# Layer 2, tiles 9 and 15: the residual of the expert output as an identity product on TensorE and a ScalarE copy, in place of a VectorE addition

## The chip, the cores and the metric

One core of one Trainium2 chip. The time is that of the device for one execution of the whole program, in microseconds (us); of several runs the median is given. The engines are called TensorE (PE in profile rows, PEld for its weight loads), VectorE (DVE), ScalarE (ACT), GpSimd (POOL) and SyncE (SP, which issues all DMA transfers here).

## The reference

Two kinds of layer alternate on x of 2048 rows by 576 columns: linear attention (32 heads) and a mixture of tiny experts. Each works on a layer-normed x and is added to x. The whole is done twice.

```python
x = x + _A_ref(_layernorm(x, axis=-1), A_wqkv, A_wo)
x = x + _B_ref(_layernorm(x, axis=-1), B_w_q, B_k1, B_k2, B_u, B_v)
x = x + _A_ref(_layernorm(x, axis=-1), A_wqkv, A_wo)
x = x + _B_ref(_layernorm(x, axis=-1), B_w_q, B_k1, B_k2, B_u, B_v)
```

The expert part, per row of x (xf is the normed row), with one expert chosen per head:

```python
q = jnp.einsum("nd,dhc->nhc", xf, w_q)
s1 = jnp.einsum("nhd,ed->nhe", q[..., :dk], k1)
s2 = jnp.einsum("nhd,ed->nhe", q[..., dk:], k2)
# best of 8 in s1 and best of 8 in s2 name one of 64 experts
act = _gelu(jnp.einsum("nd,nhkd->nhk", xf, u[top_e]))
out = jnp.einsum("nhk,nhk,nhkd->nd", g, act, v[top_e])   # g is 1: K = 1
```

The change concerns the last of the four additions, x + _B_ref, for two of the sixteen groups of rows.

## The kernel before

The 2048 rows are 16 tiles of 128. A tile goes through a number of steps, each a Python generator that is advanced piece by piece (`yield` is the boundary of a piece). In the program text, `play` holds the order as a written list: `po1.9` advances step `po` (exp_out) of layer 2 (the kernel counts layers 0 and 1), tile 9, by one piece; `x2` behind a word means two pieces. Within a part of that list, `in_order` keeps each of TensorE, ScalarE, VectorE and GpSimd to exactly that order: what stands behind a waiting instruction on its engine waits too. SyncE's queue of transfers follows its own order.

The last steps of a tile of layer 2, with the words of the list and the names in the rows:

- `O` (back_out, L483, tile ppo): TensorE multiplies the attention output by its weights, 28 matmuls. VectorE adds x in `residual` (L473) and writes x1 along with its row sum. ScalarE squares x1 (L188, junk); GpSimd makes mean and scale (L187 to L195, mb and rsb); ScalarE writes the normed row, yb (L205).
- `bc` (exp_T): TensorE transposes yb of one tile together with the expert weights cg of an earlier tile (L215, ptb: five transposes and one). ScalarE copies them out as thib (L117) and VectorE makes the rest, tlob (L118), so that products of float32 precision are made of two parts. So `bc1.12,10` transposes yb of tile 12 and cg of tile 10.
- `S` (exp_scores, L525, pps): 14 matmuls give the scores; ScalarE copies them to s (L530).
- `gel` and `sel`: ScalarE and GpSimd make the gelu, g (L539 to L545); VectorE picks the experts in a row of small operations (L553 to L590, mt to cg).
- `po` (exp_out, L609, tile po): four matmuls multiply the transposed cg by the table vmix. What remains is to add x1 and to store the result x2 to `out` (L623).

The last addition has two forms. Without a `base` step, VectorE does it in `residual` (L473), reading po and x1 and writing x2. With a `base` step ahead (exp_base, L598), TensorE first multiplies x1 by the identity matrix into the same accumulator po, the four matmuls of L609 add to it, and ScalarE copies the sum to x2 (L613). Before the change, tiles 10, 11 and 12, the last three, have this second form. All other tiles have the first.

Accumulators come from a pool `ps` of four buffers; x2 has a pool of two, so an addition or a copy waits until the output transfer of the tile before the last is done.

Of the kernel before, what the change touches and what calls it, by code (L numbers as in the profile page):

```python
# [64 lines left out]
def network(ctx, tc, x_in, wqkv, wo, wq_t, k_t, u_t, v2, c_mask, c_mask4, c_ident, c_code, c_code1, c_scale, c_shift, out):  # L65
# [90 lines left out]
    @contextmanager  # L156
    def in_order(*engines):

        ins = nc.cur_bb.bb.instructions
        last = ins[-1]  # L160
        yield
        ins = nc.cur_bb.bb.instructions
        start = next(i for i in reversed(range(len(ins))) if ins[i] is last) + 1
        for e in engines:
            mine = [i for i in ins[start:] if i.engine == e]
            for x, y in zip(mine, mine[1:]):
                tc.add_manual_dep(y, x.name, mybir.DependencyInfo(mybir.DependencyClass.NoSync, mybir.DependencyReason.DATA),
                                  reason="in_order")
# [587 lines left out]
    def play(text, at=0):  # L756

        for w in text.split():
            f, l, t, c, n = re.fullmatch(r"([A-Za-z]+)(\d)\.(-?\d+)(?:,(-?\d+))?(?:x(\d+))?", w).groups()
            run(int(l), (pieces[f], (at + int(t), at + int(c)) if c else at + int(t), int(n or 1)))  # L760
# [114 lines left out]
    with in_order(*ALL):  # L875

        play("""
            bT0.13 gel0.12 po0.11 sel0.12 v1.10 po0.11x2 gel0.12 num0.15 sel0.12 k1.10 bT0.13 v1.10 sel0.12 fT1.11
            sel0.12 oT0.14 v1.10 fT1.11 O0.14 num0.15 cT0.12 num0.15 k1.10 cT0.12 O0.14 oT0.15 bT0.13 po0.12 S0.13
            O0.14 fT1.11 S0.13 oT0.15 po0.12x3 sel0.13x2 v1.11 gel0.13 fT1.12 gel0.13 oT0.15 O0.14 sel0.13x2 k1.11  # L880
            v1.11 O0.15 fT1.12 O0.15 bT0.14 st1.10 cT0.13 v1.11 bT0.14 S0.14 cT0.13 O0.15 fT1.12 keep1.12 po0.13 k1.11
            S0.14 gel0.14 sel0.14 po0.13 gel0.14 st1.11 po0.13 k1.12 sel0.14x2 po0.13 fT1.13 k1.12 O0.15 v1.12x2
            sel0.14 v1.12 bT0.15 cT0.14x2 st1.12 fT1.13 bT0.15 po0.14 S0.15 po0.14 fT1.13 S0.15 po0.14 ldx1.1 po0.14
            ldx1.3 v1.13 fT1.14 v1.13 sel0.15x3 gel0.15 k1.13 fT1.14 gel0.15 bT0.-1 v1.13 sel0.15 cT0.15 v1.14 cT0.15
            po0.15 k1.13 q1.13 bT0.-1 po0.15 q1.13 v1.14 po0.15x2 v1.14 k1.14 wl1.0 st1.13 fT1.15x2 k1.14 k1.15 v1.15
            rl1.0 st1.14 k1.15 ldq1.13 v1.15x2 rl1.2 st1.15 lq1.0 mk1.0 zs1.0 M1.1 rl1.1 lq1.0 M1.1 rl1.3 ldx1.0 zs1.0
            M1.4x2 M1.3 lq1.1 M1.0 num1.13 num1.0 num1.13 num1.0x2 M1.3 keep1.11 lq1.1 num1.1 M1.0 oT1.0x2 num1.1
            M1.2x2 rl1.4 num1.1 num1.13 lq1.2 O1.0 oT1.1 oT1.13 q1.14 lq1.2 O1.0 oT1.1 O1.0x2 num1.2 q1.14 lq1.3x2
            num1.2 oT1.13 bc1.0,-9 num1.3 O1.1 bc1.0,-9 num1.2 S1.0 O1.1 oT1.2 S1.0 num1.3 lq1.4 gel1.0 num1.3 oT1.2
            O1.1x2 O1.2 bc1.1,-9 sel1.0 gel1.0 ldx1.2 sel1.0 lq1.4 O1.13 rl1.6 bc1.1,-9 sel1.0 num1.4x2 S1.1 O1.2x2  # L890
            ldx1.13 O1.13 S1.1 lq1.6 O1.2 sel1.0 sel1.1 bc1.2,0 rl1.5 ldx1.5 rl1.7 num1.4 oT1.3 ldq1.14 lq1.5 lq1.6
            gel1.1 bc1.2,0 oT1.4 gel1.1 sel1.1 O1.13 rl1.8 sel1.1 S1.2 po1.0 oT1.3 lq1.5 sel1.1 S1.2 O1.3 po1.0 sel1.2
            rl1.9 O1.13 oT1.4 num1.6 bc1.13,1 num1.5 sel1.2 num1.5 lq1.7 bc1.13,1 gel1.2x2 num1.5 S1.13 O1.3 lq1.7
            O1.3x2 num1.6 rl1.11 sel1.2 po1.1 oT1.5 q1.15 oT1.5 ldx1.4 sel1.2 bc1.3,2 po1.1 S1.13 gel1.13 num1.6 O1.4
            bc1.3,2 sel1.13 q1.15 ldx1.6 po1.2 O1.5 oT1.6 ldq1.15 po1.2 sel1.13 num1.14 S1.3 O1.4 lq1.8 O1.4 num1.14
            num1.7 rl1.10 sel1.13 gel1.13 O1.5 num1.14 O1.4 num1.7 S1.3 sel1.13 ldx1.7 sel1.3 oT1.6 num1.7 bc1.4,13
            ldx1.14 bc1.4,13 rl1.12 O1.6 ldx1.8 lq1.8 po1.13 O1.5 gel1.3 O1.5 sel1.3 oT1.7 po1.13 sel1.3 num1.8 O1.6
            S1.4 gel1.3 num1.8 oT1.7 S1.4 sel1.3 sel1.4 gel1.4 sel1.4 oT1.14 bc1.5,3 lq1.9 O1.6 sel1.4 bc1.5,3 S1.5
            po1.3 ldx1.15 O1.6 num1.8 ldx1.11 gel1.4 oT1.8 oT1.14 num1.15 S1.5 sel1.4 bc1.6,4 po1.3 sel1.5 gel1.5
            lq1.9 bc1.6,4 num1.15 O1.14 num1.9 oT1.8 S1.6 O1.14x2 sel1.5 O1.14 S1.6 gel1.5 po1.4 num1.15 sel1.5x2 O1.7  # L900
            po1.4 num1.9 gel1.6 bc1.14,5 O1.7 bc1.14,5 oT1.15 gel1.6 O1.7 sel1.6 num1.9 O1.8 po1.5 S1.14x2 O1.7 po1.5
            oT1.9 sel1.6 O1.8 sel1.6 ldx1.9 O1.8 sel1.6 sel1.14 gel1.14 oT1.15 sel1.14 lq1.10 oT1.9 lq1.10 bc1.7,6x2
            O1.9 gel1.14 O1.8 sel1.14 po1.6 ldx1.10 po1.6 num1.10 S1.7x2 sel1.14 num1.10 O1.9 sel1.7 bc1.8,14 num1.10
            lq1.11 bc1.8,14 po1.14 sel1.7 O1.9 lq1.11 O1.9 gel1.7x2 sel1.7 S1.8 sel1.7 O1.15 S1.8 ldx1.12 gel1.8
            sel1.8 num1.11 po1.14 O1.15 oT1.10 bc1.9,7 gel1.8 sel1.8 bc1.9,7 lq1.12 O1.15 S1.9 sel1.8 oT1.10 num1.11
            sel1.8 lq1.12 O1.15 num1.12 po1.7 S1.9 num1.11 bc1.15,8 gel1.9 po1.7 sel1.9 O1.10 gel1.9 oT1.11 num1.12
            bc1.15,8 O1.10x2 po1.8x2 sel1.9 oT1.11 S1.15x2 sel1.9 O1.11 O1.10 gel1.15 sel1.9 gel1.15 sel1.15 bc1.10,9
            num1.12 O1.11 sel1.15 bc1.10,9 O1.11 oT1.12 S1.10 sel1.15 po1.9 O1.11 sel1.15 oT1.12 S1.10 gel1.10
            bc1.11,15 sel1.10 O1.12 po1.9 gel1.10 bc1.11,15 O1.12x2 S1.11 sel1.10x2 po1.15 sel1.10 po1.15 S1.11
            sel1.11 O1.12 sel1.11 base1.10 bc1.12,10x2 gel1.11x2 sel1.11 S1.12x2 sel1.11 base1.11 gel1.12 sel1.12  # L910
            gel1.12 po1.10 bc1.-1,11x2 base1.12 sel1.12x2 po1.10 sel1.12 po1.11x2 bc1.-1,12x2 po1.12x2
        """)
# [44 lines left out]
```

## Time and profile before

| | |
|---|---|
| runs | 719.56, 718.05, 720.6 us; median 719.56 us |
| profiled execution | 718.14 us, its span 716.4 us |
| granted TensorE clock, mean | 0.996 |
| TensorE busy | 699.6 us (98%) |
| VectorE busy | 475.1 us (66%) |
| ScalarE busy | 321.6 us (45%) |
| GpSimd busy | 201.6 us (28%) |
| identity products L598, weight loads and matmuls | 12 each, 697.7 to 706.5 us |
| ScalarE copies L613 | 3, of 0.65 us each |

The span runs from the first to the last instruction; the time of the execution has 1.74 us more. A busy share says how long an engine had work, not whether the end waited for it. In rows of the timeline the columns are start, duration, engine, line, operation, output and inputs, shapes, count, and in brackets the idle time of that engine just before with what ended it. The mean over all stages hides that the last 30 us have few tiles left to overlap.

### The profile page before, as it was taken

What the parts mean: (1) busy time and instruction counts of PE and PEld (TensorE: products, weight loads), DVE (VectorE), ACT (ScalarE), POOL (GpSimd) and SP (SyncE); (2) the same over time, 40 slices, a digit from 0 to 9 for tenths busy, and PEclk for the clock granted to TensorE, in tenths of its full rate; (3) what the DMA queues carried; (4) which work ended last, traced back from release to release, by engine and by line L of the source; (5) the groups of instructions that cost most, each with busy time, mean ns of one, the idle gap of its engine ahead of it and who ended that gap; (6) DMA issues with size and microseconds to landing.
All of it is one profiled execution on the core that took longest, in us unless ns stands there. A gap on an engine that the chain in (4) does not pass through costs nothing.

```text
span 716.4 us, 14695 instructions
## 1 busy us (share of the span) xinstructions
PE 699.6 (98%) x5464; PEld 650.7 (91%) x5464; DVE 475.1 (66%) x1031; ACT 321.6 (45%) x658; POOL 201.6 (28%) x543
## 2 busy tenths in 40 slices
PE   9999999999999999999999999999999999999995
PEld 6999989999998999899998999899899999899984
DVE  5533343435437877688787888551647788988996
ACT  5422422343224456455565554644544534454442
POOL 3211000111004533334443433210323234434431
PEclk9999999999999999999999999999999999999998
DMA  9847777765302322566767665514532324111101
GB/s 270 291 164 243 266 234 262 247 192 175 108 1 64 103 101 91 162 216 215 245 218 233 212 196 175 168 44 128 149 120 84 97 86 125 47 67 34 67 17 66
DMA packets 82711, 107.17 MB, mean 150 GB/s; under 512 B 8976, under 2 KB 47376, under 8 KB 82640
## 3 DMA queue, kind: packets, MB, share of 16 engines
q1 hardware_dynamic: 82640, 106.24, 46.5%
q8 instruction: 43, 0.70, 0.4%
q14 instruction: 28, 0.23, 0.1%
HBM read 68.88 MB, written 37.32 MB: 148 GB/s over the span
## 4 chain that ended last, share of the span: by engine, by line
PE 82%; DVE 8%; ACT 4%; issue 2%; DMA 2%; POOL 1%; SPq 0%; DVEq 0%; ACTq 0%; POOLq 0%
PE ppk L258 15%; PE ppv L258 14%; PE ppq L258 14%; PE ppo L483 12%; PE pps L525 7%; PE kva L525 5%; PE kva L360 3%; PE fold_ps L641 2%; PE po L609 2%; PE ptb L215 2%; PE m L414 1%; PE pto L215 1%; DVE x L473 1%; PE ppq L270 1%; PE ppk L270 1%
## 5 line engine op out<-in xcount | busy, mean ns | idle before, releaser
L483 PE MATMUL ppo<-ohi,thio 126*128 126x252 f32 (+1 forms) x320 | 50.5, 300 | 2.6 <-ACT thio L117 2.6
L483 PEld LDWEIGHTS ppo<-ohi,thio 126*128 126x128 f32 (+1 forms) x320 | 44.8, 189 | 4.4 <-ACT thio L117 3.1
L258 PE MATMUL ppk<-whi,thif 128*128 128x252 f32 (+1 forms) x300 | 45.3, 298 | 0.8 <-ACT thif L117 0.8
L188 ACT ACTIVATE junk<-x,mb 128x576 bf16<-128x576 f32 x32 | 24.8, 775 | 45.2 <-POOL mb L187 44.9
L453 POOL TENSOR_TENSOR o<-pq,zb 128x576 f32<-128x576 f32 x19 | 27.4, 1441 | 62.2 <-ACT zb L399 58.6
L258 PE MATMUL ppv<-whi,thif 128*128 128x252 f32 (+1 forms) x300 | 44.7, 295 | 0.1
L258 PEld LDWEIGHTS ppk<-whi,thif 128*128 128x128 f32 x300 | 40.9, 188 | 4.0 <-issue 2.9
L205 ACT ACTIVATE yb<-x,rsb 128x640 f32<-128x640 f32 x32 | 29.5, 921 | 33.3 <-POOL rsb L195 33.3
L179 POOL TENSOR_SCALAR rsf<-mvf 128x1 f32<-128x1 f32 x16 | 3.4, 212 | 145.3 <-DVE mvf L176 145.2
L258 PE MATMUL ppv<-whi,tlof 128*128 128x252 f32 (+1 forms) x300 | 43.9, 293 | 0.0
L258 PE MATMUL ppk<-whi,tlof 128*128 128x252 f32 (+1 forms) x300 | 43.9, 293 | 0.0
L258 PEld LDWEIGHTS ppv<-whi,thif 128*128 128x128 f32 x300 | 41.3, 188 | 1.0 <-issue 0.4
L258 PEld LDWEIGHTS ppk<-whi,tlof 128*128 128x128 f32 x300 | 41.2, 188 | 0.0
L258 PEld LDWEIGHTS ppv<-whi,tlof 128*128 128x128 f32 x300 | 41.2, 188 | 0.0
L483 PE MATMUL ppo<-olo,thio 126*128 126x252 f32 (+1 forms) x256 | 39.6, 293 | 0.0
L258 PE MATMUL ppq<-whi 128*128 128x252 f32 (+1 forms) x260 | 39.5, 299 | 0.0
L483 PE MATMUL ppo<-ohi,tloo 126*128 126x252 f32 (+1 forms) x256 | 39.4, 293 | 0.0
L277 DVE TENSOR_SCALAR ek<-ek 128x576 f32<-128x576 f32 x16 | 7.3, 457 | 46.4 <-ACT ek L276 46.4
L258 PEld LDWEIGHTS ppq<-whi 128*128 128x128 f32 x260 | 36.0, 188 | 0.6 <-DVE eq L287 0.3
L483 PEld LDWEIGHTS ppo<-olo,thio 126*128 126x128 f32 x256 | 36.2, 188 | 0.0
L483 PEld LDWEIGHTS ppo<-ohi,tloo 126*128 126x128 f32 x256 | 36.1, 188 | 0.0
L258 PE MATMUL ppk<-wlo,thif 128*128 128x252 f32 x240 | 36.1, 293 | 0.0
(205 smaller groups left out, 1784.6 us busy)
## 6 DMA issues: line engine op xcount, KB each, us to landing
fold<-in_wq_t SPq DMA_DIRECT2D x64, 288.0 KB
whi<-hl_d SPq DMA_DIRECT2D x26, 320.0 KB
y_df<-rf SPq DMA_DIRECT2D x23, 320.0 KB
gf<-y_df SPq DMA_DIRECT2D x92, 80.0 KB
pq_d<-eq SPq DMA_DIRECT2D x19, 288.0 KB
pq<-pq_d SPq DMA_DIRECT2D x19, 288.0 KB
xf<-in_x SPq DMA_DIRECT2D x16, 288.0 KB
x<-in_x SPq DMA_DIRECT2D x16, 288.0 KB
```

Of the source, the lines that this page charges most:

```text
L188: nc.scalar.activation(junk, xt, AF.Square, bias=m[:, 0:1], accum_out=m[:, 1:2])
L205: nc.scalar.activation(y, x2, AF.Identity, scale=rs[:, 0:1], bias=rs[:, 1:2])
L215: nc.tensor.transpose(pt[:, b * P:(b + 1) * P], x, ident)
L258: nc.tensor.matmul(o[:, at:at + c1 - c0], tt[a == "lo"][:, b, :], wb[:, cols + c0:cols + c1], start=(i == 0), stop=(i == len(todo) - 1))
L270: nc.tensor.matmul(p[:, at:at + c1 - c0], tt[a == "lo"][:, b, :], wb[:, cols + c0:cols + c1], start=(i == 0), stop=(i == len(todo) - 1))
L277: nc.vector.tensor_scalar(e, e, 1.0, EPS, op0=ALU.min, op1=ALU.add)
L360: nc.tensor.matmul(a[64 * h:64 * h + 64, c * 72:c * 72 + n], vt[:, 2 * c + h], fk[:, f0:f0 + n], start=(t == 0 and c == 0), stop=(t == NT ...
L453: nc.gpsimd.tensor_tensor(o[:, :D], pq, zb, op=ALU.mult)
L483: nc.tensor.matmul(p[:, at:at + c1 - c0], hl[a][:r, b], w[:r, c0:c1], start=(i == 0), stop=(i == len(todo) - 1))
L525: nc.tensor.matmul(p[:, :512], hl[a == "lo"][:, b, :], shi[:, b] if w == "hi" else slo[:, blocks(REM)[b][1]], start=(i == 0), stop=(i == l ...
L609: nc.tensor.matmul(p[:, at:at + c1 - c0], c[i], vmix[:, c0:c1], start=(i == 0 and not based), stop=(i == 1))
L641: nc.tensor.matmul(p[32 * j:32 * j + 32, at:at + c1 - c0], kpad[:, ch // 2, 24 - 8 * a:56 - 8 * a], st[:, c0:c1], start=(a == 0), stop=(a ...
```

## The change

Two words are added to the list: `base1.9` directly ahead of `po1.9`, and `base1.15` directly ahead of `po1.15`. exp_out then finds a base and takes its second form for tiles 9 and 15.

```diff
-            num1.12 O1.11 sel1.15 bc1.10,9 O1.11 oT1.12 S1.10 sel1.15 po1.9 O1.11 sel1.15 oT1.12 S1.10 gel1.10
-            bc1.11,15 sel1.10 O1.12 po1.9 gel1.10 bc1.11,15 O1.12x2 S1.11 sel1.10x2 po1.15 sel1.10 po1.15 S1.11
+            num1.12 O1.11 sel1.15 bc1.10,9 O1.11 oT1.12 S1.10 sel1.15 base1.9 po1.9 O1.11 sel1.15 oT1.12 S1.10 gel1.10
+            bc1.11,15 sel1.10 O1.12 po1.9 gel1.10 bc1.11,15 O1.12x2 S1.11 sel1.10x2 base1.15 po1.15 sel1.10 po1.15 S1.11
```

Per tile this adds two instructions in the program on TensorE (each becomes two weight loads and two matmuls in the trace), removes one addition with its row sum from VectorE, and adds one copy on ScalarE.

In the instruction order, names carry the tile in the middle (`po_15_9296` is po of tile 15). TensorE around tile 15, before; pps_11 are the scores of tile 11, ptb_12 the transposes of tile 12:

```order
L525 MATMUL pps_11_9266<-shi,tlob_11_9214 128x512 x5
L609 MATMUL po_15_9296<-vmix,thib_11_9213 128x252
L609 MATMUL po_15_9296<-vmix,thib_11_9213 128x324
L609 MATMUL po_15_9296<-vmix,tlob_11_9214 128x252
L609 MATMUL po_15_9296<-vmix,tlob_11_9214 128x324
L598 MATMUL po_10_9331<-x_10_9020,ident 128x252
L598 MATMUL po_10_9331<-x_10_9020,ident 128x324
L215 MATMUL ptb_12_9334<-ident,yb_12_9322 128x128 x5
```

And after:

```order
L525 MATMUL pps_11_9267<-shi,tlob_11_9216 128x512 x5
L598 MATMUL po_15_9297<-x_15_8830,ident 128x252
L598 MATMUL po_15_9297<-x_15_8830,ident 128x324
L609 MATMUL po_15_9297<-vmix,thib_11_9215 128x252
L609 MATMUL po_15_9297<-vmix,thib_11_9215 128x324
L609 MATMUL po_15_9297<-vmix,tlob_11_9216 128x252
L609 MATMUL po_15_9297<-vmix,tlob_11_9216 128x324
L598 MATMUL po_10_9333<-x_10_9020,ident 128x252
L598 MATMUL po_10_9333<-x_10_9020,ident 128x324
L215 MATMUL ptb_12_9336<-ident,yb_12_9324 128x128 x5
```

The identity product of tile 15 now stands between the scores of 11 and po of 15; that of tile 9 stands likewise between the scores of 10 and po of 9.

ScalarE from the gelu of tile 10 to thib of tile 12, before:

```order
L539 ACTIVATE g_10_9202<-s_10_9174 128x64
L543 ACTIVATE g_10_9202<-g_10_9202 128x64
L117 ACTIVATE thib_11_9213<-ptb_11_9206 128x768
L188 ACTIVATE junk,mb_12_9263<-x_12_9260,mb_12_9263 128x576
L530 ACTIVATE s_11_9281<-pps_11_9266 128x512
L205 ACTIVATE yb_12_9322<-x_12_9260,rsb_12_9318 128x640
L117 ACTIVATE thib_12_9341<-ptb_12_9334 128x768
```

And after:

```order
L539 ACTIVATE g_10_9204<-s_10_9174 128x64
L613 ACTIVATE x_9_9253<-po_9_9182 128x576
L543 ACTIVATE g_10_9204<-g_10_9204 128x64
L117 ACTIVATE thib_11_9215<-ptb_11_9208 128x768
L188 ACTIVATE junk,mb_12_9264<-x_12_9261,mb_12_9264 128x576
L613 ACTIVATE x_15_9309<-po_15_9297 128x576
L530 ACTIVATE s_11_9282<-pps_11_9267 128x512
L205 ACTIVATE yb_12_9324<-x_12_9261,rsb_12_9320 128x640
L117 ACTIVATE thib_12_9343<-ptb_12_9336 128x768
```

The copy of tile 9 stands between the two gelu operations of tile 10, the copy of tile 15 ahead of s of 11 and yb of 12. On VectorE the addition of tile 9 is gone from between the selection of 10 (m_10) and tlob of 11, that of tile 15 from between cg of 10 and mt of 11. SyncE's queue keeps its order; the transfers of tiles 9 and 15 now wait for ScalarE.

## The prediction

> **What bounds the kernel now.** I read the page's chain of work that ended last first.
>
> ```profile
> PE 82%; DVE 8%; ACT 4%; issue 2%; DMA 2%; POOL 1%; SPq 0%; DVEq 0%; ACTq 0%; POOLq 0%
> ```
>
> TensorE is the bound over the whole run. The change, though, touches only the last 30 us, so what matters is that stretch, and there I read the chain in order of time (start, duration, engine, tile, line).
>
> ```profile
> 659.22 3.66 PE ppo L483 x28
> ...
> 689.02 0.54 PE po L609 x4
> 689.56 0.66 PE ptb L215 x6
> 690.22 0.04 issue
> 690.25 3.92 PE ppo L483 x28
> 694.18 3.27 PE pps L525 x14
> 697.45 0.53 PE po L609 x4
> 697.99 0.97 PE po L598 x4
> 698.96 0.88 PE ptb L215 x6
> ...
> 699.92 0.82 ACT thib L117
> 700.74 0.04 issue
> 700.78 3.56 PE pps L525 x14
> ...
> 712.59 0.65 ACT x L613
> ```
>
> The first row is for comparison. By the program's order the pieces from 689.02 on are po of tile 9, ptb of 11, ppo of 12, pps of 11, po of 15, the identity product (L598) of tile 10, ptb of 12, thib of 12, pps of 12 and, after s and the selection of 12, the last copy. Two things are to be seen. From 689 to 699.8 TensorE runs without a gap worth naming: whatever is inserted there is paid. From ptb of 12 on, each step waits for the one before it (transposes, ScalarE's thib, scores, ScalarE's s, VectorE's selection, output): whatever delays ptb of 12 delays the end by the same amount. Both identity products of the change go into the first stretch, and both copies onto the engine that has to feed ptb of 12.
>
> ScalarE's own rows around the place, in order of time, with its idle time in brackets:
>
> ```profile
> 691.83 0.26 ACT L543 ACTIVATE g<-g 128x64 f32<-128x64 f32 x1 [1.34 <-POOL g L541]
> 691.99 0.80 ACT L117 ACTIVATE thib<-ptb 128x768 fp32r<-128x768 f32 x1
> ...
> 697.49 0.60 ACT L530 ACTIVATE s<-pps 128x512 f32<-128x512 f32 x1 [1.21 <-PE pps L525]
> 697.98 0.91 ACT L205 ACTIVATE yb<-x,rsb 128x640 f32<-128x640 f32 x1
> ```
>
> The s at 697.49 is that of tile 11; it starts when pps of 11 ends. The yb at 697.98 is tile 12's normalized input, and its end at 698.89 is what ptb of 12 begins on. ScalarE takes its rows in order: thib of 11 had its transposes at 690.22 (chain) and still stood until 691.99, behind a g that waited for GpSimd.
>
> **The change, part by part.** *Identity product of tile 9, TensorE.* In the chain an identity product is one piece of 0.97 us (697.99). It goes ahead of po of 9: po ends at 689.02 + 0.97 + 0.54 = 690.53, ptb of 11 at 691.19. Before, ppo of 12 stood 0.04 us for ScalarE's s of 10 and then took 3.92 us; the piece at 659.22, which follows its predecessor without a wait, took 3.66, and I take 3.68. That wait is over by 691.19, so ppo of 12 ends at 691.19 + 3.68 = 694.87 in place of 694.18: of the 0.97 us, 0.69 remain.
>
> *Copy of tile 9, ScalarE, and its addition off VectorE.* In ScalarE's order it stands between the two g rows of tile 10. It can start at about 690.57 and takes 0.65 us (the copy at 712.59); the second g did not start before 691.83, since GpSimd was late. It fits in that 1.34 us gap: nothing. It would begin to cost if po of 9 came over 0.6 us later still. On VectorE the addition goes:
>
> ```profile
> 692.26 0.74 DVE L473 SCALAR_TENSOR_TENSOR x<-po,x 128x576 f32<-128x576 f32 x1
> 694.22 0.76 DVE L473 SCALAR_TENSOR_TENSOR x<-ppo,x 128x576 f32<-128x576 f32 x1 [0.33 <-PE ppo L483]
> 698.18 0.75 DVE L473 SCALAR_TENSOR_TENSOR x<-po,x 128x576 f32<-128x576 f32 x1
> 698.86 0.42 DVE L553 TENSOR_TENSOR mt<-s 128x256 f32<-128x256 f32 x1
> 705.06 0.43 DVE L553 TENSOR_TENSOR mt<-s 128x256 f32<-128x256 f32 x1 [0.17 <-ACT s L530]
> ```
>
> After it, the residual of 12 (694.22) already waited 0.33 us for TensorE's ppo, which now ends 0.69 us later. The 0.74 us freed turn into more waiting. That residual also starts the layer norm of tile 12, whose scale yb reads. The row of yb at 697.98 has no idle time ahead of it, so the scale was there by then; 0.69 us later is 698.67 at the latest, ahead of the time at which ScalarE comes to yb below, and costs nothing more.
>
> *Identity product of tile 15, TensorE.* pps of 11 now runs 694.87 to 698.14; the new product ends at 699.11, po of 15 (0.53) at 699.64, the product of tile 10 at 700.61. On TensorE alone that makes 0.69 + 0.97 = 1.66 us at ptb of 12.
>
> *Copy of tile 15, ScalarE: the added wait.* The new order puts it ahead of s of 11 and yb of 12. It waits for po of 15, which TensorE does 1.5 us after pps of 11, and both s and yb queue behind it, though their inputs are there (pps of 11 at 698.14, the scale by 698.67). Start after the product and spacing of consecutive ScalarE operations of this width come from these rows:
>
> ```profile
> 667.81 0.65 ACT L284 ACTIVATE eq<-ppq 128x576 f32<-128x576 f32 x1 [1.35 <-PE ppq L258]
> 668.36 0.65 ACT L285 ACTIVATE ppq<-ppq 128x576 f32<-128x576 f32 x1
> ...
> 707.05 0.53 PE L609 MATMUL po<-vmix,tlob 128*128 128x252 f32 x2
> ...
> 707.62 0.65 ACT L613 ACTIVATE x<-po 128x576 f32<-128x576 f32 x1 [0.64 <-PE po L609]
> ```
>
> A copy starts 0.04 us after its product ends (707.58 to 707.62), and the next operation 0.55 us after it starts. So the copy of 15 starts at 699.64 + 0.04 = 699.68, s of 11 at 700.23, and yb of 12 another 0.49 (697.49 to 697.98) later at 700.72, against 697.98 before: 2.74 us. ptb of 12 moves with it, from 698.96 to 701.70, and TensorE stands idle from 700.61 to 701.70.
>
> *Addition of tile 15 off VectorE.* It stood between the selection of 10 and mt of 11, 0.75 us that mt of 11 no longer waits for; but mt of 11 reads s of 11, which now ends at 700.83, so VectorE is 2.0 us later there than at 698.86. That hides: tlob of 12 and the selection of 11 are needed 2.74 us later, and mt of 12 at 705.06 waited 0.17 us for ScalarE's s even before. VectorE's two removed additions, 0.74 + 0.75 us of work, therefore return nothing.
>
> *The output transfers* are issued when the copies end: tile 9's about 1.8 us earlier than before, tile 15's about 1.4 us later. Their queue has nothing behind them before the copy of tile 10. That copy and the next reuse their buffers some 10 us later; the last transfer of all, after the copy that ends at 713.24, was done by the span's end at 716.4. Nothing.
>
> *Sum:* 2.74 us on the serial tail. *Bounds:* a copy that names several transfers' semaphores may need small steps on ScalarE's sequencer; and the price of a product can be read in other ways:
>
> ```profile
> L613 ACTq EVENT_SEMAPHORE  x6: 17/38/1699, 706.0 to 710.8; - x6
> ...
> 704.16 1.13 PE L598 MATMUL po<-x,ident 128*128 128x252 f32 x4
> 704.88 0.67 PE L609 MATMUL po<-vmix,thib 128*128 128x252 f32 x2
> ```
>
> A product from its start to the next one's start is 0.72 us, to its own modelled end 1.13; I keep 0.97, since the next row there was lengthened by the queue (0.67, where the pair of this shape at 707.05 took 0.53). Two products give −0.50 or +0.32. Five semaphore steps of 38 ns give up to +0.19, ScalarE without overlap up to +0.21 (0.65 + 0.60 for 0.55 + 0.49). So 2.24 to 3.46.
>
> The profiled execution took 718.14 us, 1.42 below the median of 719.56; the sum on it is 720.88. The next measurement should be like the median, so I forecast 719.56 + 2.74 = 722.3.
>
> **Rivals.**
>
> *ScalarE doesn't hold the tail.* If s and yb got past the copy's wait, TensorE's 1.66 us alone would count: 721.2. The thib row at 691.99 speaks against it. Chance 0.07.
>
> *VectorE's relief decides: faster.* VectorE has little idle time in its rows above, and both additions stood in its queue ahead of selections. If the end hung on that queue, 1.49 us would go: 719.56 − 1.49, about 718.1. It decides from the point where mt of 12 begins at the end of the selection of 11 and not on s of 12. The row at 705.06 shows it waiting for ScalarE, and the two products are on TensorE's gapless stretch. Chance 0.04.
>
> *The products hide.* Should TensorE's rows hold slack that the modelled ends conceal, and the copy too start early, the time stays 719.6. The 0.04 us ahead of ppo of 12 and what its restart cost are all that I see of it. Chance 0.05. That the change might not do what it says is excluded by the order of the program.
>
> *The clock falls.* In the tail TensorE stood for 2.75 us up to 710.33, and the granted clock (the number behind the five engines) fell:
>
> ```profile
> 710.33 0.48 PE L215 MATMUL ptb<-ident,cg 128*128 128x128 f32 x1 [2.75 <-DVE cg L590]
> ```
>
> ```profile
> 708.00:710.00 2.00, 0.00 (x0) 0.00 (x0) 1.76 (x6) 0.27 (x1) 0.00 (x0) 1.00 0.70 267
> 710.00:712.00 2.00, 1.30 (x4) 1.01 (x5) 0.57 (x2) 0.28 (x1) 0.00 (x0) 0.58 0.00 0
> ```
>
> The changed kernel opens a gap of 1.1 us before ptb of 12, and the gap of 0.94 us before pps of 12 follows after 0.88 us of transposes: 2.0 us idle in 2.9. If that lowered the clock to 0.58 for pps of 12, its 3.27 us would grow by 2.4, and the time would be 724.7. Two gaps shorter than 2.75 with work between them speak against it. Chance 0.04. [...]
>
> **How the numbers follow.** The forecast's case has 0.80. The range goes from the profiled 718.14 + 1.66 = 719.8 (TensorE alone, on the profiled execution) to the slowest run 720.6 + 3.46, rounded down, 724.0. About 0.3% (2.16 us) is what a measurement of this kernel can tell from no change, and 2.74 is close above it: runs of before spread over 2.5 us, so I give one in seven of the forecast's cases to "same". Slower: 0.80 × 0.85 + 0.04 + a quarter of 0.07, 0.74. Same: 0.12 + 0.05 + 0.04, 0.21. Faster: 0.05.
>
> **What would show it.** Right: in the trace after, ppo of 12 ends about 0.7 us later, ScalarE's copy of 15 starts about 1.5 us after pps of 11 ends and waits for L609, s of 11 and yb of 12 follow directly, ptb of 12 starts about 2.7 us later with an idle gap on TensorE that yb ends, and every row from there keeps its distance to the end. VectorE's mt of 11 then waits for ScalarE. Wrong: ptb of 12 later by 1.7 us or less with no gap ahead of it; mt of 12 waiting for nothing; a granted clock below 1.00 in pps of 12; or a copy of 9 that pushes thib of 11 and with it pps of 11.

## The result and the profile after

| | runs | median, us | range, us |
|---|---|---|---|
| before | 6 | 719.39 | 718.05 to 720.6 |
| after | 6 | 723.62 | 720.89 to 727.19 |

The ratio is 1.0061 (95% interval 1.0045 to 1.0076): slower by some 4.2 us, where 2.74 had been forecast. A second comparison of the same two kernels on another chip (the run again, below) gave 1.0049 (1.0037 to 1.0061), 3.7 us between the medians. The profiled execution of after took 723.72 us, its span 721.9 us; that is 5.58 us more than the one of before.

The chain of the kernel after, in order of time, from the scores of tile 10 (columns: start, duration, engine, tile, line):

```profile
686.81 3.28 PE pps L525 x14
...
692.25 3.66 PE ppo L483 x28
695.91 3.27 PE pps L525 x14
699.19 0.97 PE po L598 x4
700.16 0.55 PE po L609 x4
...
700.73 0.65 ACT x L613
701.38 0.49 ACT s L530
701.87 0.81 ACT yb L205
...
702.73 0.89 PE ptb L215 x6
...
703.65 0.32 issue
703.98 0.82 ACT thib L117
...
704.84 5.08 PE pps L525 x14
...
718.17 0.65 ACT x L613
```

For comparison, the same first piece in the chain of before; its later pieces are in the prediction:

```profile
685.75 3.27 PE pps L525 x14
```

The chain now leaves TensorE between po of tile 15 and ptb of 12: copy of 15, s of 11, yb of 12, all on ScalarE. That is the mechanism that was forecast. Measured from the start of the scores of tile 10, the pieces stand later than before by:

| piece | before | after | later by |
|---|---|---|---|
| end of ppo of 12 | 8.43 | 9.10 | 0.67 |
| ptb of 12 | 13.21 | 15.92 | 2.71 |
| thib of 12 | 14.17 | 17.17 | 3.00 |
| pps of 12 | 15.03 | 18.03 | 3.00 |
| last copy | 26.84 | 31.36 | 4.52 |

So the 5.58 us are 2.71 up to ptb of 12, 0.29 more at thib of 12, 1.52 more inside the scores of 12 (5.08 us in place of 3.56), and 1.06 that came earlier in the program, ahead of every changed row (686.81 against 685.75). These 1.06 belong to the execution and not to the change: four profiled executions of the changed kernel began the scores of 10 at 686.81, 686.67, 685.51 and 687.15.

ScalarE's, VectorE's and TensorE's rows at the places of the forecast, from the timeline of after (idle time ahead in brackets):

```profile
691.63 0.65 ACT L613 ACTIVATE x<-po 128x576 f32<-128x576 f32 x1
692.88 0.26 ACT L543 ACTIVATE g<-g 128x64 f32<-128x64 f32 x1 [0.60 <-POOL g L541]
...
700.73 0.65 ACT L613 ACTIVATE x<-po 128x576 f32<-128x576 f32 x1 [2.72 <-PE po L609]
```

```profile
701.97 0.43 DVE L553 TENSOR_TENSOR mt<-s 128x256 f32<-128x256 f32 x1 [1.97 <-ACT s L530]
```

```profile
702.73 0.77 PE L215 MATMUL ptb<-ident,yb 128*128 128x128 f32 x5 [1.06 <-ACT yb L205]
```

The copy of 9 sits in the gap before the second g, which still waits 0.60 us for GpSimd. The copy of 15 finds ScalarE idle for 2.72 us. VectorE's mt of 11 waits 1.97 us for ScalarE, and TensorE stands 1.06 us ahead of ptb of 12.

What was not in the forecast's sum is the 0.29 us at thib of 12 and, larger, the long pps of 12. The windows of after around it (length; busy time and count on PE, PEld, DVE, ACT, POOL; granted clock; DMA share, GB/s):

```profile
702.02:705.43 3.41, 1.46 (x9) 1.14 (x10) 3.20 (x9) 1.61 (x3) 0.33 (x2) 1.00 0.24 89
705.43:708.84 3.41, 3.41 (x10) 2.64 (x9) 2.37 (x7) 0.26 (x1) 1.15 (x4) 0.50 0.00 0
```

For 3.41 us (705.43 to 708.84), while TensorE was busy throughout, the granted clock (the number behind the five engines) was 0.50. This is the fourth rival, which had been given a chance of 0.04.

### The profile page after: what moved, and what is told of

Same layout as the page of the kernel before. It is cut to its first block, busy times and chain, and to the rows that moved or that the text cites. A ratio compares the mean times of both kernels' runs of the same rounds, so it can differ in the third digit from the quotient of the medians.

```text
span 721.9 us, 14708 instructions
## 1 busy us (share of the span) xinstructions
PE 702.6 (97%) x5472; PEld 653.2 (90%) x5472; DVE 472.3 (65%) x1027; ACT 322.7 (45%) x660; POOL 201.9 (28%) x543
## 4 chain that ended last, share of the span: by engine, by line
PE 78%; DVE 9%; ACT 4%; DMA 3%; issue 3%; POOL 1%; SPq 1%; DVEq 0%; ACTq 0%; POOLq 0%
PE ppq L258 14%; PE ppk L258 13%; PE ppv L258 13%; PE ppo L483 12%; PE pps L525 8%; PE kva L525 5%; PE kva L360 3%; PE fold_ps L641 2%; PE po L609 2%; PE ptb L215 2%; PE m L414 1%; DMA go<-y_do 1%; DMA wst<-in_wqkv 1%; DVE x L473 1%; PE pto L215 1%
## 5 line engine op out<-in xcount | busy, mean ns | idle before, releaser
L258 PE MATMUL ppv<-wlo,thif 128*128 128x252 f32 x240 | 36.1, 293 | 0.0
```

The lines of the kernel that those rows point to most:

```text
L258: nc.tensor.matmul(o[:, at:at + c1 - c0], tt[a == "lo"][:, b, :], wb[:, cols + c0:cols + c1], start=(i == 0), stop=(i == len(todo) - 1))
```

## Experiments

Two questions: does each half of the change cost what its step says, and is the slow pps of 12 made by TensorE's gap (the clock) or by something that the products and copies bring with them? All positions below count from the start of the scores of tile 10 in the same profile, as in the table above; "later" is against before.

**One half at a time.** The first kernel has only the word of tile 9, the second only that of tile 15.

```diff
 # only tile 9 (against before)
-... S1.10 sel1.15 po1.9 O1.11 ...
+... S1.10 sel1.15 base1.9 po1.9 O1.11 ...
 # only tile 15 (against before)
-... sel1.10x2 po1.15 sel1.10 po1.15 S1.11
+... sel1.10x2 base1.15 po1.15 sel1.10 po1.15 S1.11
```

> Only tile 9 has the identity product and the copy. My theory: ppo of 12 ends 0.7 us later against its own pps of 10 and so does ptb of 12; TensorE has no new gap ahead of ptb of 12, so the granted clock stays 1.00 through pps of 12 (3.5 us). Against before: +0.7 us. A rival in which the identity products themselves, and not the gap, bring the clock down: pps of 12 takes about 5 us and the time is +2 us or more.

> Only tile 15 has the identity product and the copy. My theory: +0.97 us on TensorE and 1.1 us more because yb of 12 stands behind the copy, so ptb of 12 moves 2.05 us against pps of 10, with a gap of about 1.1 us ahead of it; that gap lets the granted clock fall in pps of 12 in most executions, which adds up to 1.8 us. Against before: +2.0 to +3.9, about +3.5 in the median. The rival in which the extra 1.8 us come from elsewhere in the run: +2.0 and clock 1.00.

Chain of the kernel with tile 9 alone, then of that with tile 15 alone:

```profile
686.88 3.31 PE pps L525 x14
...
700.79 0.88 PE ptb L215 x6
...
702.61 3.55 PE pps L525 x14
```

```profile
687.62 3.34 PE pps L525 x14
...
702.87 0.89 PE ptb L215 x6
...
704.71 5.07 PE pps L525 x14
```

Tile 9 alone puts ptb of 12 at 13.91, later by 0.70; its copy costs nothing. Tile 15 alone puts it at 15.25, later by 2.04. The two sum to 2.74. The times are 719.97 us, ratio 1.0001 (0.9989 to 1.0013), too coarse for 0.7 us, and 722.43 us, ratio 1.0038 (1.0024 to 1.0052). Both stand against a median of 719.53 for before, 33 runs on that chip, as do the next two. pps of 12 took 5.07 us with tile 15, 3.55 with tile 9: what stretches it belongs to tile 15.

**The copy out of the way.** Both products stay, but the list lets s of 11 and yb of 12 go ahead of the copy of 15.

```diff
 # against after
-... base1.15 po1.15 sel1.10 po1.15 S1.11
-            sel1.11 O1.12 sel1.11 base1.10 ...
+... base1.15 po1.15 sel1.10 S1.11
+            sel1.11 O1.12 po1.15 sel1.11 base1.10 ...
```

> Both products as in the changed kernel, but the copy of tile 15 stands behind yb of 12 on ScalarE. My theory: s of 11 and yb of 12 no longer wait for it, ptb of 12 follows the product of tile 10 without a gap, TensorE's 1.66 us remain and the clock stays: +1.7 us against before, and about 2.5 us less than the changed kernel. The rival in which the products alone make the loss: as the changed kernel, +4.

Its chain, and the copy in ScalarE's timeline, which now follows yb:

```profile
687.64 3.30 PE pps L525 x14
...
701.55 0.97 PE po L598 x4
702.52 0.67 PE ptb L215 x6
...
704.41 3.56 PE pps L525 x14
```

```profile
700.57 0.92 ACT L205 ACTIVATE yb<-x,rsb 128x640 f32<-128x640 f32 x1
701.58 0.65 ACT L613 ACTIVATE x<-po 128x576 f32<-128x576 f32 x1
```

ptb of 12 stands at 14.88, later by 1.67: TensorE's own work alone, against 1.66 in the prediction. It follows the product of tile 10 (701.55 + 0.97) with no gap, and pps of 12 is 3.56 us again. Time 721.63 us, ratio 1.0028 (1.0012 to 1.0044). The rest of the 2.71 us is thus the copy's place in ScalarE's order, and the long pps goes with the gap.

**The gap filled.** The changed kernel, with the product of tile 10 computed twice into the same accumulator (the first result is overwritten), so that TensorE has 0.97 us more work exactly where it stood idle.

```diff
 # against after, in exp_base
+        for spare in (True, False)[0 if (l, t) == (1, 10) else 1:]:
-        for c0, c1, at in PARTS:
+            for c0, c1, at in PARTS:
-            nc.tensor.matmul(..., start=True, stop=False)
+                nc.tensor.matmul(..., start=True, stop=spare)
```

> The changed kernel with the identity product of tile 10 computed twice, so that TensorE works through the gap ahead of ptb of 12. My theory: ptb of 12 starts no later than in the changed kernel, the clock stays at 1.00 through pps of 12 (3.5 us, not 5.1), and the time is the mechanical part alone: +2.7 us against before, about 1.5 less than the changed kernel although 0.97 us of work were added. The rival without the clock: no gain, +4.2, or +5 if the added work counts.

Its chain, then the doubled product in TensorE's timeline:

```profile
687.62 3.30 PE pps L525 x14
...
703.56 0.89 PE ptb L215 x6
...
705.67 3.56 PE pps L525 x14
...
717.34 0.65 ACT x L614
```

```profile
701.36 2.10 PE L599 MATMUL po<-x,ident 128*128 128x252 f32 x8
```

ptb of 12 stands at 15.94, later by 2.73, as in after (2.71) although TensorE does more: the ScalarE row sets it. pps of 12 takes 3.56 us at full clock, and the last copy is later by 2.88 in place of 4.52. In the traces, the tail with more work on TensorE was shorter than that of an execution that lost its clock. One profile alone could be chance; the last section adds how busy TensorE was around that place. The time does not resolve it: 722.74 us, ratio 1.0041 (1.0027 to 1.0055), an interval that overlaps those of after.

**The changed kernel again**, on the chip of the stall kernel and the two tail kernels below (before there: 719.17 us, 29 runs).

> The changed kernel once more, for a larger number of executions beside the granted clock of each. My theory: executions with a mean granted clock of about 0.993 (one stretch of 3.4 us at half clock in pps of 12) take about 1.6 us more than those with 0.996 to 0.998, and the latter lie at +2.7 us against before. The rival in which the excess comes from the start of the run or from transfers: the time does not go with the clock.

The windows of this execution, up to the fall and after it:

```profile
700.80:704.21 3.41, 1.62 (x9) 0.84 (x8) 2.19 (x6) 2.11 (x4) 0.00 (x0) 1.00 0.23 87
704.21:707.62 3.41, 2.90 (x7) 2.35 (x8) 3.14 (x9) 0.86 (x3) 1.47 (x5) 0.50 0.01 2
```

722.87 us, ratio 1.0049 (1.0037 to 1.0061). ptb of 12 was later by 2.73. The clock fell again, but at 704.21, before pps of 12 began: pps took 4.84 us, and the clock was 1.00 again from 708 to 716 us and 0.97 in the mean from 716 to 718: the last po took 0.87 us, where before had 0.50 from 710.33 on and took 1.35. The last copy is later by 3.68 in this execution, against 4.52 in the first.

**The gap without products and copies.** Before, with two squares of x1 of tile 12 into a scrap tile put into ScalarE's order between s of 11 and yb of 12.

```diff
 # against before
+    def stall(l, t):
+        for i in range(2):
+            nc.scalar.activation(junk, xs["b", l, t], AF.Square)
-... po1.15 S1.11
+... po1.15 S1.11 stall1.12
```

> The kernel before with two more ScalarE passes (Square of x1 of tile 12 into junk, unused) ahead of yb of 12: no identity product and no copy added, only yb late by 2 x 0.55 us. My theory: ptb of 12 moves by 1.1 us with a gap of 1.1 us ahead of it, and in a part of the executions the clock falls to half in pps of 12 as in the changed kernel: +1.1 us with the clock up, +2.7 with it down, about +1.5 in the median. The rival in which the new identity products bring the clock down: +1.1 and never 0.993 more often than before.

720.92 us, ratio 1.0028 (1.0014 to 1.0042). ptb of 12 was later by 1.29, yet in this profile pps of 12 still took 3.56 us: no fall. Taken alone that spoke against the gap as the cause. The second execution of this kernel, below, had the fall.

**Single executions.** Two more profiled executions of the changed kernel and one of the stall kernel, unaltered.

> The changed kernel, one profile, to see whether there are executions in which the clock stays up. My theory: yb of 12 and ptb of 12 are 2.7 us later against pps of 10 than in the kernel before, in every execution; pps of 12 takes either 3.5 us (clock 1.00) or 4.8 to 5.1 (clock 0.50 for 3.4 us), depending on where the stretches of 3.4 us happen to begin. A rival in which the change always brings the clock down: always about 5 us.

> As the look before it: 2.7 us at ptb of 12 every time; pps of 12 at 3.5 us or at 4.8 to 5.1 us, according to chance.

> The stall alone, once more, one profile: ptb of 12 1.2 to 1.3 us later than before against pps of 10; my theory lets pps of 12 take about 5 us here as well in some executions, though no identity product was added. The rival in which the added products bring the clock down: 3.5 us always.

The first took 722.39 us; ptb of 12 was later by 2.74, pps of 12 took 5.02 us, and the last copy was later by 4.50. The second took 722.56 us; its chain:

```profile
687.15 3.27 PE pps L525 x14
...
703.09 0.89 PE ptb L215 x6
...
705.21 3.56 PE pps L525 x14
...
717.01 0.65 ACT x L613
```

ptb of 12 is later by 2.73, pps of 12 takes 3.56 us, and the last copy is later by 3.02: the forecast's case, with the 0.29 us at thib of 12 on top (2.73 + 0.29 = 3.02). The same program, in the same place, loses its clock in one execution and keeps it in another. The third, the stall kernel (720.61 us), from TensorE's timeline:

```profile
700.66 0.76 PE L215 MATMUL ptb<-ident,yb 128*128 128x128 f32 x5 [1.28 <-ACT yb L205]
702.43 2.50 PE L525 MATMUL pps<-shi,thib 128*128 128x512 f32 x5 [0.90 <-ACT thib L117]
```

Its pps of 12 took 4.97 us in the chain. No identity product and no copy was added here. So the clock fell with a gap alone too, in one of two executions here.

**Trying to use it.** If clock lost to gaps costs time, the last gap of before, 2.75 us ahead of the last ptb, where its clock fell to 0.50, could be filled. One kernel puts ten spare matmuls on scrap data there (nine are in its trace), at the end of po of 11; another also puts yb of 12 ahead of s of 11 on ScalarE, and the identity product of tile 10 behind the transposes of yb of 12, into TensorE's wait for thib.

```diff
 # first, against before
+    def tail_warm(l, t):
+        p = psum(f"warm{l}_{t}")
+        for i in range(t):
+            nc.tensor.matmul(p[:, :512], junk[:, :P], junk[:, :512], start=True, stop=True)
-... po1.11x2 bc1.-1,12x2 po1.12x2
+... po1.11x2 wm1.10 bc1.-1,12x2 po1.12x2
 # second, against the first
-... po1.15 sel1.10 po1.15 S1.11
-            sel1.11 O1.12 sel1.11 base1.10 bc1.12,10x2 gel1.11x2 ...
+... po1.15 sel1.10 po1.15 O1.12
+            S1.11 sel1.11x2 bc1.12,10 base1.10 bc1.12,10 gel1.11x2 ...
```

> The kernel before with ten matmuls of junk on TensorE in the idle stretch of 2.75 us ahead of the last transposes; their result is not used. My theory: the clock stays at 1.00 to the end, the last transpose and the last four matmuls shrink from 0.49 and 1.35 us to about 0.27 and 0.54: -1.0 us against before. The rival in which the junk delays the transposes, or the clock falls all the same: 0 or slower.

> The kernel before with the junk matmuls of the run before, with yb of 12 ahead of s of 11 on ScalarE, and with the identity product of tile 10 behind ptb of 12, where TensorE waits for thib. My theory: ptb of 12 starts up to 0.3 us earlier, the gap ahead of pps of 12 is filled: -1.2 to -1.3 us against before. The rival in which the new gap ahead of ptb of 12 (up to 0.7 us) costs the clock: slower than the run with the junk alone.

The first kernel's timeline at the end, TensorE and then VectorE:

```profile
707.36 2.11 PE L630 MATMUL warm<-junk 128*128 128x512 bf16 x9
...
710.80 0.55 PE L609 MATMUL po<-vmix,thib 128*128 128x252 f32 x2 [0.37 <-ACT thib L117]
```

```profile
710.78 0.29 DVE L118 TENSOR_TENSOR tlob<-ptb,thib 128x128 fp32r<-128x128 f32 x1 [0.79 <-ACT thib L117]
```

The granted clock was 1.00 from 706 to 714 us, and the last po took 0.87 us (710.80 to 711.67) in place of the 1.35 of before; its second half has to wait for VectorE's tlob, which ends at 711.07, so it could not get shorter. The last copy is 0.55 us earlier, at 26.29, about half of what was hoped for. The time, 719.13 us, ratio 1.0003 (0.9988 to 1.0018), shows nothing of it. The second missed altogether: 719.5 us, ratio 1.0003 (0.9989 to 1.0017). Its chain says why:

```profile
699.98 0.92 ACT yb L205
700.90 0.49 ACT s L530
...
701.48 0.44 DVE mt L553
...
707.44 0.44 DVE mt L553
```

Counted from its scores of tile 10 (688.00), yb came only 0.25 us earlier (11.98 for 12.23), s of 11 came behind it, and with s VectorE's mt of 11 was 0.37 us later (13.48 for 13.11 in before, where it is at 698.86). The selections of 11 and 12 now stand back to back on VectorE and are the bound. No version beat the kernel before.

## Why the prediction was right in its mechanism and short in its size

*Identity product of 9: 0.97 us, of which 0.69 remain.* Right: 0.67 at the end of ppo of 12 (its wait of 0.04 us is gone, and it took 3.66 us in place of 3.92), and 0.70 with that half alone.

*Copy of 9: nothing.* Right. The half alone carries no more than its product, and g still waits 0.60 us.

*Product of 15: 1.66 us on TensorE together.* Right: 1.67 with the copy moved away.

*Copy of 15 ahead of s and yb: 2.74 us at ptb of 12.* Right: 2.71, 2.73, 2.74 and 2.73 in four executions, with the gap of 1.06 us where 1.1 was worked out. The first rival (1.66 only, ScalarE not holding the tail) is excluded by the kernel with the gap filled: 0.97 us more on TensorE did not move ptb of 12.

*VectorE's relief returns nothing.* Right. mt of 11 waits 1.97 us and mt of 12 waits for ScalarE's s:

```profile
710.64 0.43 DVE L553 TENSOR_TENSOR mt<-s 128x256 f32<-128x256 f32 x1 [2.60 <-ACT s L530]
```

*"Every row from there keeps its distance to the end."* Here it failed, in two places. The smaller: thib of 12 starts 1.25 us after ptb of 12 and not 0.96, in all four executions of after and with the gap filled, but not in before, in the halves or in the stall kernel (0.91 to 0.97). The profile puts the wait under "issue" (0.32 us), with nothing that it shows to end it. The same 0.32 us stands in the chain of the late copy, so it comes in all six profiled executions with both products and copies, and not from the gap; its cause stays open.

The larger is the clock. The step that failed is the sentence that weighed the fourth rival: "Two gaps shorter than 2.75 with work between them speak against it." It took the one fall in the trace of before as if a single long gap was needed. No gap of 2.75 us was needed here: with gaps of 1.06 us ahead of ptb of 12 and 1.24 ahead of pps of 12, and work between them, the clock fell in three of four profiled executions of the changed kernel. In the window of after that ends at the fall, 702.02 to 705.43, lie the last 0.71 us of the first gap and all of the second; TensorE was busy for 1.46 us of it. The rival's price was too high as well: 2.4 us supposed a clock of 0.58 until pps had done its 3.27 us of work, but the half clock lasted 3.41 us in after, in which a clock of 0.50 loses half, 1.71 us, and in the run again it began before pps did. It cost 1.52 and 1.48 us in two executions; 0.66 in a third, where the clock was 1.00 for the last po in turn (3.68 − 3.02); and none in the fourth. With 3.02 us for the rest, a mean over the four of 0.92 makes 3.9, between the two measured 4.2 and 3.7. That 723.62 lies inside the range of 719.8 to 724.0 is in part luck: its top was made of the slowest run of before and of bounds on other terms, none of them the clock.

The mean granted clock that comes with each execution's time points the same way, but coarsely, since it also holds the fall at the very end. Of the five profiled executions that lost their clock around pps of 12, three have 0.993, but two have 0.995 and 0.996, so a limit of 0.994 counts too few:

| kernel, single executions left out | executions | at 0.994 or less | their mean time, us | at 0.996 to 0.998, us |
|---|---|---|---|---|
| after | 11 | 4 | 724.64 | 722.64 |
| tile 15 alone | 12 | 4 | 723.48 | 721.89 |
| stall only | 12 | 2 | 724.18 | 720.91 |
| gap filled | 10 | 1 | | |
| tile 9 alone, late copy, both tail kernels | 48 | 0 | | |
| before | 62 | 5 | 722.4 | 719.33 |

Kernels with the gap are at 0.994 or less in 10 of 35 executions, kernels that have no gap or a filled one, before among them, in 6 of 120. Where the five of before lost theirs no trace shows. Against before, the changed kernel's executions without the low clock are 3.3 us slower, near the 3.02 of the trace; those with it 5.3 us.

## What to carry to other kernels

On an engine that takes its rows strictly in order, an operation costs the wait for its inputs, not its 0.65 us: look at what stands behind it and who waits for that. Moving work off an engine that was waiting anyway returned nothing here (0.74 + 0.75 us of VectorE), and of the work added to TensorE in its gapless stretch 0.70 of 0.97 us was paid for tile 9 and all 0.97 for tile 15 (1.67 − 0.70). When a change opens a gap on TensorE, look in the trace at TensorE's busy time over the stretch of 3.41 us ahead of a fall (here 1.62 us or less), not at the length of one gap alone, and price the lower clock as a case that comes in some executions (three of four here). With the gap filled the clock was 1.00 here, by nine spare matmuls at the end of before and by a product computed twice in the changed kernel, in one profile each.

## What the runs showed of the hardware

In the trace of after the granted clock went down at 705.43, up at 708.84 and down at 715.67: 3.41 and 6.83 us apart, one and two times the same length. In the other profiled executions with a fall around pps of 12 the clock of 0.50 lasted as long: from 704.21 to 707.62 in the run again, 705.10 to 708.51 with tile 15 alone, 703.42 to 706.83 in the first single execution, and some 3.4 us (702.2 to 705.6) in the second of the stall kernel. So these traces are laid out here in stretches of 3.41 us, counted from a change, and TensorE's busy time in a stretch is set beside what the clock did at its end. Below are one stretch of before (followed by the fall); two of the execution of the changed kernel that kept its clock; one of the stall kernel's first execution and one of its second (no fall after either):

```profile
706.92:710.33 3.41, 0.67 (x5) 0.32 (x4) 3.05 (x11) 0.72 (x2) 0.53 (x1) 1.00 0.46 173
```

```profile
700.56:703.97 3.41, 2.34 (x14) 1.54 (x12) 1.53 (x4) 1.94 (x3) 0.00 (x0) 1.00 0.23 87
703.97:707.38 3.41, 2.17 (x9) 1.81 (x10) 3.24 (x9) 1.21 (x3) 1.45 (x5) 1.00 0.01 2
```

```profile
699.97:703.38 3.41, 2.20 (x11) 1.50 (x10) 3.13 (x10) 2.65 (x4) 0.82 (x2) 1.00 0.10 40
```

```profile
709.01:712.43 3.42, 1.64 (x8) 1.08 (x7) 3.25 (x10) 1.61 (x4) 1.11 (x3) 1.00 0.29 112
```

The first number after the length is TensorE's busy time, 0.67 us ahead of the fall in before. Ahead of the other falls it was 1.46 us (702.02 to 705.43) and 0.90 us (712.26 to 715.67) in after, 1.38 us with tile 15 alone (701.70 to 705.10), 1.24 us in the first single execution (700.02 to 703.43) and 1.62 us, 47%, in the run again (700.80 to 704.21). In the stretches shown without a fall it was 2.34, 2.17, 2.20 and 1.64 us, the last 48%. Before and after have together some 400 stretches at full clock, counted back from their falls; three were followed by a fall, and the least busy of the others had some 2.0 us in each (300.73 to 304.15, 299.24 to 302.66). Since the ends of matmuls are modelled and a few records can be missing, 1.62 and 1.64 are not to be told apart; that other kernels would fall at the same busy time is not shown. The clock stayed at 0.50 after a stretch at that clock with 1.81 us busy (before, 710.33 to 713.75) and was 1.00 after one with 2.90 us (again, above) and one with 3.41 us (after, 705.43 to 708.84).

On this reading the same gap costs or does not according to where such a stretch ends. How often that is can be estimated from the traces, if every position is taken as equally likely and 1.63 us, between the two numbers above, as the limit: around the gap, a stretch of 3.41 us has less than that busy at some 37% of the positions in the changed kernel, 34% in the stall kernel and 29% with tile 15 alone, an estimate from TensorE's rows in after, in the second execution of the stall kernel and with tile 15 alone. Three falls in four profiled executions are more than the share. By it the fall costs some 0.45 us in the mean (37% of 1.22, the mean of 1.52, 1.48 and 0.66), and the change 3.5 us, an estimate. In before, with tile 9 alone, with the late copy and with the gap filled there is no such position (the least is 2.45, 2.45, 2.17 and 2.08 us).

The first fall in after came without a long gap: the stretch of after from 702.02 to 705.43 held none longer than 1.24 us.
